# Linear attention into a mixture of experts on one core: rows kept whole per batch, one load for v's last tokens, an earlier choice of experts, and shifted tile addresses

## The chip, the core and the metric

The kernel runs on one core of a Trainium2 chip. The metric is the time of one execution in device microseconds (us); less is better. Several runs were timed, and one more execution was recorded by the hardware profiler.

## What is computed

The reference has two halves. The first is attention with a feature map, for 8 batches of 8 heads with 576 tokens and a head size of 64; the second sends the resulting 4608 rows of 512 numbers to one of 8 experts each.

```python
def phi(x):                                   # (.., 64) -> (.., 256)
    proj = x @ w_phi                          # 64 -> 128
    proj = proj - max(abs(proj))              # over the 128
    return concat([exp(proj), exp(-proj)])
kv = phi(k)^T @ v;  z = sum over tokens of phi(k)
attn = (phi(q) @ kv) / (phi(q) @ z + 1e-6)    # per batch and head
x = attn as rows of (batch, token), 512 wide
out = x.copy()
for rows with x @ w_skip > 0:                 # the others stay as they are
    e = argmax(x @ w_gate);  g = softmax(x @ w_gate)[e]
    out += g * (relu(x @ w1[e]) @ w2[e])      # w1: 512x1024, w2: 1024x512 per expert
```

## The kernel before

**Attention.** The work is cut into 16 units: a unit is four heads of one batch (`hq` is 0 or 1, `b` the batch), once for k and once for q. A loop over steps `t` from 0 to 38 runs a software pipeline: step 2g loads unit g, and each unit takes two steps. Within a step, the letters of `CFG['order']` say in which order projections (L336), maxima and subtractions (L346, L347 on VectorE, giving `m` and `u`), exponentials (L361, L378 on ScalarE), the products with v (L417, into `ps_K`) and the products of q with the result (L482, L535) are written. In the steps between `CFG['man']` that is the order on TensorE, VectorE, ScalarE and GpSimd; outside them, and for the DMA queue of SyncE (SP) throughout, a scheduler sets it. Each engine and each queue works strictly in its order.

**Loads.** For each unit SP issues four loads of v (L301, tile `v`, one buffer), four of k (L289), eight of q (L293), and four small ones with tokens 16 and 17 of each row of v straight into the tile `vt` (L308). GpSimd copies `v` into `vm` (L312), where a column of ones makes z.

**Rows and their choice of expert.** `norm` (L457 to L467) divides and writes two things: the rows, in `xm` (512 tokens) and `xt` (the last tokens of a pair of batches), and partial scores in `lgm`, `lgt`. There is one `xm` for each half row (`hq`). `store_rows` writes it to the scratch array `xrows`, `store_out` to the output. `post(b)` then works through a batch's choice in stages that are put off by whole steps: `best`, `exps`, `hot`, `gates` (which writes token number and gate into the last two columns of the row, L605 and L607), `store_rows`; then `rank`, `index`, `store_out`. Helpers put off in this way wait in `later` and are run at the letters L and R.

**Early experts.** After the sixth batch (`EB` is 5) `pick(0)` and `pick(1)` (from L700) take the two fullest experts so far; their numbers go to `eid`, their rows are gathered by GpSimd (L217, tile `xg`), and SP can issue the first loads of expert weights (L188 for w1, L191 for w2, tile `wraw_c`). ScalarE copies each block of weights (L199), and GpSimd or VectorE takes the remainder (L204). After attention come ten groups of expert slots; the tables for all but the first three are made once every batch has been ranked (L1068).

Of the kernel before, what the change touches and what calls it, by code (L numbers as in the profile page):

```python
# [20 lines left out]
CFG = {'late': 1, 'gp': (0, 1, 2, 4, 6, 8, 9, 11, 12, 14, 17, 19, 21), 'rows': 9.0, 'tab': (2, 4, 5, 6, 6, 7, 8, 9, 10, 11, 12, 13, 16, 20, 32), 'ql': 0, 'cp': 0, 'seq': ('E', 'E', 'E', 'C', 'C', 'SC', 'C', 'DS', 'C', 'D'), 'post': (2, 4, 1), 'man': (3, 36), 'eng': ('PE', 'DVE', 'Activation', 'Pool'), 'nb': {'K': 1, 'O': 1, 'A': 2, 'P': 3, 'U': 2}, 'apools': (('ld', 2), ('hl', 4), ('up', 5), ('zp', 2), ('ep', 7), ('kvp', 5), ('ac', 1), ('xp', 3)), 'mpools': (('rawp', 1), ('mx', 2), ('wseta', 1), ('mo', 2), ('wsetb', 1), ('wsetc', 1), ('rawq', 1)), 'lag': (2, 2, 3, 0), 'order': ('Lv12KQebRcdBuExzwl', 'L01aKQ2ebRcdBuExwzy'), 'vl': 0, 'at': 1, 'eb': (2, 2), 'ub': 4, 'stage': (1, 1, 2, 2), 'dve': ('0', '1', 'ntkq', '2', 'n2', 'tkq', 'n2t'), 'pd': 1, 'vq': 0, 'qq': 1, 'xb': 4, 'whole': 'k'}
# [3 lines left out]
def kernel(  # L25
# [106 lines left out]
    mark = const.tile([1, 32], I32, name="mark")[:, 0:1]  # L132
# [98 lines left out]
    with actx:  # L231
# [65 lines left out]
        def st_loadv(u):  # L297
            u.v0 = ld.tile([P, 4, 4 * D], F32, tag="v", name="v", bufs=1)
            u.vt = vts[u.g % len(vts)]
            for q4 in range(4):  # L300
                nc.sync.dma_start(  # L301
                    out=u.v0[q4 * 32:q4 * 32 + 32].rearrange("p h (t c) -> p h t c", c=D),
                    in_=vv[u.g][:, :, 4 * q4:4 * q4 + 4, :],
                )
            for pr in range(2):
                for q2 in range(2):
                    r = pr * 64 + q2 * 32
                    (nc.scalar if CFG["vq"] else nc.sync).dma_start(out=u.vt[r:r + 32, pr, :, 0:D], in_=vv[u.g][:, 2 * pr:2 * pr + 2, 16 + q2, :])  # L308

        def st_v(u):  # L310
            u.v = vms[u.g % len(vms)]
            nc.gpsimd.tensor_copy(out=u.v[:, :, :, 0:D], in_=u.v0.rearrange("p h (t c) -> p h t c", c=D))  # L312

# [157 lines left out]
        def st_use_q(u, pr, th):  # L471
            if th == 0:
                u.os = xp.tile([P, 8, NAUG], F32, tag="os", name="os", bufs=2)
            kva = kva_of[u.g]
            ov = bank("O")[:, 0:4 * NAUG].rearrange("p (t c) -> p t c", c=NAUG)
            e = u.e[pr]
            h0 = u.hq * 4 + 2 * pr
            for j in range(2):
                for hd in range(2):
                    for half in range(2):  # L480
                        for s in range(2):
                            nc.tensor.matmul(  # L482
                                ov[s * 64:s * 64 + 64, 2 * j + hd, :], e[:, half, s, 4 * hd + 2 * th + j],
                                kva[:, half, 2 * pr + hd, :], start=(half == 0), stop=(half == 1),
                            )
            nc.scalar.activation(out=u.os[:, 4 * th:4 * th + 4], in_=ov, func=AF.Copy)  # L486
            if th == 0:
                return
            if pr == 0:

# [4 lines left out]

            def finish():
                if pr == 0:
                    return
# [6 lines left out]
            norms.append(norm(u.os, 8, xm[:, :, pr * 2 * D:(pr + 1) * 2 * D].rearrange("p a (h d) -> p a h d", d=D),  # L505
                              lgm[:, :, h0:h0 + 2, :], 4) + [finish])

        def store_rows(b, hq):
# [1 line left out]
            nc.sync.dma_start(out=rowm[b][:, :, c], in_=xm_of[b * NQ + hq])  # L510
            if b % 2 == 1:
                nc.sync.dma_start(out=rowt[b // 2][:, c], in_=xt_of[b // 2, hq][:, 0])

        def store_out(b, hq):
            c = slice(hq * 4 * D, (hq + 1) * 4 * D)
            for q4 in range(4):
                rr = slice(q4 * 32, q4 * 32 + 32)
                nc.sync.dma_start(out=outv[b][:, q4 * 4:q4 * 4 + 4, c], in_=xm_of[b * NQ + hq][rr, :, 0:4 * D])
            if b % 2 == 1:
                for par in range(2):  # L520
                    for q2 in range(2):
                        rr = slice(par * 64 + q2 * 32, par * 64 + q2 * 32 + 32)
                        nc.sync.dma_start(out=outv[b - 1 + par][:, 16 + q2, c], in_=xt_of[b // 2, hq][rr, 0, 0:4 * D])
# [27 lines left out]
        def post(b):  # L551
            last = b == B - 1
            xm, lgm = xm_of[b * NQ + 1], lg_of[b]
            t0 = 9 * (b // 2) + 4 * (b % 2)
# [48 lines left out]
            def gates():  # L603
                for xx, lg, o, n in parts:
                    nc.scalar.activation(  # L605
                        out=xx[:, :, HW[1] - 1:HW[1]], in_=sid[:, t0 + o:t0 + o + n].rearrange("p (t o) -> p t o", o=1), func=AF.Copy)
                    nc.vector.reciprocal(out=xx[:, :, HW[1] - 2:HW[1] - 1], in_=gt[:, o:o + n].rearrange("p (t o) -> p t o", o=1))  # L607

            if last:
# [140 lines left out]
        for t in range(NPR + F + LQ + 2):  # L750
# [36 lines left out]
            for c in CFG["order"][t % 2]:  # L787
# [603 lines left out]
```

## Time and profile before

| | |
|---|---|
| times of three runs | 634.76 us median, 632.61 to 641.91 |
| the profiled execution | 632.63 us, of which the span of instructions is 630.9 us |
| mean granted TensorE clock | 0.947 |
| busy share | TensorE 85%, VectorE 71%, ScalarE 54%, GpSimd 48% |
| moved by DMA | 117.38 MB in 158466 packets |

The span is the time from the first to the last instruction of the core; some 1.7 us of the execution lie around it. In rows of the profile, PE is TensorE, PEld its weight loads, DVE VectorE, ACT ScalarE, POOL GpSimd, and SPq the DMA queue that SyncE issues. L301 is line 301 of the kernel before. A row of waits names who waited, for whom, the sum in us, how often, and the longest. In a timeline each row has the start and the length in us, the instruction, how many were merged, and in brackets the idle time ahead of it with what ended it.

### The profile page before, as it was taken

The page shows a single profiled execution, that of the slowest core. Times are in us where ns is not written, and L with a number is a line of the kernel's source. Part 1 is how long each engine was busy: PE and PEld are TensorE (multiplying, and loading weights), DVE is VectorE, ACT ScalarE, POOL GpSimd, SP SyncE. Part 2 cuts the span into 40 slices and gives each one's busy share as a digit, 9 for nine tenths or more (in the row PEclk, how much of TensorE's full clock was granted, in tenths as well). Part 3 has the DMA queues.
Part 4 walks back from the last instruction along what each step waited for, and adds up shares of the span by engine and source line. Part 5 has one row for each costly group of instructions (what it writes and reads, how often), then busy time and mean ns, then how long its engine had stood idle before and what let it go on. Part 6 is the DMA issues. An engine that isn't in the chain of part 4 may idle for free. (4 is left out here: it accounts for less than half of the span.)

```text
span 630.9 us, 20820 instructions
## 1 busy us (share of the span) xinstructions
PE 539.2 (85%) x8638; PEld 498.9 (79%) x8638; DVE 448.5 (71%) x781; ACT 341.7 (54%) x574; POOL 305.1 (48%) x502
## 2 busy tenths in 40 slices
PE   2679999888988869888975888879999988999994
PEld 2679899878987869787875777669988968888893
DVE  3687788876867847776755389986787788857751
ACT  1257677656754647566545353434567755664720
POOL 3112233535425144343246955996386956559021
PEclk9789999998998979989888798979999999999998
DMA  7877777777877688858734967478767788767500
GB/s 150 178 155 149 152 166 146 153 199 161 197 160 164 153 176 175 199 124 180 189 101 135 316 186 267 136 242 267 229 202 239 241 291 282 245 219 266 205 19 28
DMA packets 158466, 117.38 MB, mean 186 GB/s; under 512 B 88355, under 2 KB 139683, under 8 KB 158370
## 3 DMA queue, kind: packets, MB, share of 16 engines
q1 hardware_dynamic: 150304, 105.93, 63.9%
q0 software_dynamic: 3200, 9.45, 4.3%
q8 instruction: 69, 1.13, 0.8%
q10 hardware_dynamic: 4866, 0.66, 0.7%
q14 instruction: 27, 0.22, 0.1%
HBM read 92.77 MB, written 24.02 MB: 185 GB/s over the span
## 5 line engine op out<-in xcount | busy, mean ns | idle before, releaser
L204 POOL TENSOR_TENSOR w<-wraw_c,w 128x256 fp32r<-128x256 f32 x124 | 116.8, 973 | 35.4 <-ACT w L199 35.3
L346 DVE TENSOR_REDUCE m<-ps_A 128x8 f32<-128x1024 f32 x64 | 77.1, 1204 | 59.1 <-PE ps_A L336 59.1
L199 ACT ACTIVATE w<-wraw_c 128x1024 fp32r<-128x1024 f32 x96 | 98.1, 1051 | 20.2 <-DMA wraw_c<-in_moe_w_dram 20.1
L204 DVE TENSOR_TENSOR w<-wraw_c,w 128x1024 fp32r<-128x1024 f32 x65 | 85.9, 1333 | 11.4 <-ACT w L199 11.1
L336 PE MATMUL ps_A<-wsrc,xT 64*128 64x128 f32 x1024 | 80.8, 309 | 14.5 <-DVE u L347 13.1
L336 PEld LDWEIGHTS ps_A<-wsrc,xT 64*128 64x128 f32 x1024 | 73.1, 217 | 17.4 <-DVE u L347 13.3
L482 PE MATMUL ps_O<-kva,eq 128*64 128x74 f32 x2048 | 81.3, 233 | 5.9 <-ACT os L486 5.9
L417 PE MATMUL ps_K<-vm,ek 128*64 128x65 f32 x2048 | 79.6, 223 | 3.9 <-ACT ek L361 2.7
L347 DVE TENSOR_TENSOR u<-ps_A,m 128x1024 f32<-128x1024 f32 x64 | 78.4, 1225 | 4.0
L482 PEld LDWEIGHTS ps_O<-kva,eq 128*64 128x64 f32 x2048 | 72.8, 140 | 10.3 <-ACT os L486 6.1
L378 ACT ACTIVATE eq<-ps_V 128x1024 f32<-128x1024 f32 x64 | 65.7, 1028 | 21.5 <-PE ps_V L369 21.5
L417 PEld LDWEIGHTS ps_K<-vm,ek 128*64 128x64 f32 x2048 | 72.9, 140 | 4.8 <-issue 4.0
L1015 PE MATMUL ps_O<-w,hh 128*128 128x512 f32 x160 | 64.4, 403 | 2.5 <-DVE o L962 2.5
L361 ACT ACTIVATE ek<-u 128x1024 f32<-128x1024 f32 x64 | 64.1, 1056 | 2.3 <-DVE u L347 2.3
L948 POOL DMA_INDIRECT out_dram<-o,si x22 | 29.9, 1358 | 55.8 <-DVE si L947 49.2
L486 ACT ACTIVATE os<-ps_O 128x296 f32<-128x296 f32 x64 | 26.8, 419 | 46.8 <-PE ps_O L482 46.4
L312 POOL COPY vm<-v 128x1024 f32<-128x1024 f32 x16 | 16.6, 1037 | 71.2 <-DMA v<-in_v_dram 59.6
L1019 PE MATMUL ps_O<-w,hh 128*128 128x512 f32 x120 | 48.0, 400 | 3.2 <-POOL w L204 3.2
L1020 PE MATMUL ps_O<-w,hlo 128*128 128x512 f32 x120 | 47.6, 397 | 0.0
L465 POOL TENSOR_TENSOR xm<-os,rec 128x512 f32<-128x512 f32 x32 | 33.4, 1044 | 18.6 <-DVE rec L464 18.0
L1002 PE MATMUL ps_P<-x,w 128*128 128x256 f32 x144 | 37.1, 290 | 4.7 <-DVE x L879 4.7
L325 DVE STREAM_TRANSPOSE xT<-raw 128x512 f32<-128x512 f32 x64 | 40.4, 668 | 0.0
(269 smaller groups left out, 1106.2 us busy)
## 6 DMA issues: line engine op xcount, KB each, us to landing
wraw_c<-in_moe_w_dram SPq DMA_DIRECT2D x96, 512.0 KB, 4.6
raw<-in_k_dram SPq DMA_DIRECT2D x64, 280.0 KB, 5.8
raw<-in_q_dram SPq DMA_DIRECT2D x120, 72.0 KB, 5.1
v<-in_v_dram SPq DMA_DIRECT2D x64, 128.0 KB, 3.0
out_dram<-xm SPq DMA_DIRECT2D x64, 128.0 KB, 3.2
xrows<-xm SPq DMA_DIRECT2D x8, 516.0 KB, 5.0
xrows<-xm SPq DMA_DIRECT2D x8, 512.0 KB, 4.8
vt<-in_v_dram SPq DMA_DIRECT2D x64, 16.0 KB, 3.0
```

Source lines behind the costliest of these rows:

```text
L199: nc.scalar.activation(out=hi, in_=raw, func=AF.Copy)
L204: eng.tensor_tensor(out=lo[:, r], in0=raw[:, r], in1=hi[:, r].bitcast(F32), op=ALU.subtract)
L336: nc.tensor.matmul(p[:, hd, j * NF:(j + 1) * NF], xT[r], wsrc[r], start=True, stop=True)
L346: lambda: nc.vector.tensor_reduce(out=m, in_=pv, axis=AX.X, op=ALU.max, apply_absolute_value=True),
L347: lambda: nc.vector.tensor_tensor(out=uu, in0=pv, in1=m.rearrange("p h (j o) -> p h j o", o=1).broadcast_to([P, 2, n, NF]), op=ALU.subtract),
L361: nc.scalar.activation(out=o, in_=uu, func=AF.Exp, scale=(1.0, -1.0)[a])
L378: return [lambda a=a: nc.scalar.activation(out=e[:, a].rearrange("p s g c -> p s (g c)"), in_=t, func=AF.Exp, scale=(1.0, -1.0)[a]) for a ...
L417: nc.tensor.matmul(o[s * 64:s * 64 + 64, hd, half, :], e[:, half, s * 64:s * 64 + 64], x, start=(g == 0), stop=(g == 4))
L482: nc.tensor.matmul(ov[s * 64:s * 64 + 64, 2 * j + hd, :], e[:, half, s, 4 * hd + 2 * th + j], kva[:, half, 2 * pr + hd, :], start=(half == ...
L1015: nc.tensor.matmul(y[sub], hh[:, t], wh[:, fi, :], start=first, stop=False)
L1019: nc.tensor.matmul(y[sub], hh[:, t], wl[:, fi, :], start=False, stop=False)
L1020: nc.tensor.matmul(y[sub], hlo[:, t], wh[:, fi, :], start=False, stop=last)
```

## The change

1. **One tile of rows for each batch.** `xm` is 514 columns wide and allocated once per batch; `xt` likewise once per pair. A batch's rows go to `xrows` in one store (128 runs of 8,224 bytes in place of 1,024 runs of about 1 KB), and to the output in four stores in place of eight. Nothing is stored any more when only the first half is done.
2. **v's last tokens.** The four loads into `vt` become one load into a new tile `v1` on 32 partitions, and four GpSimd copies from there.
3. **Half steps.** `now` counts half steps, and a new letter `r` at the end of a step runs what is due there. All batches but the sixth keep their distances (`post` (4, 8, 2) for (2, 4, 1), and so on); the sixth has distances of its own: `post` starts half a step after its rows in place of a whole one, the stages follow after 1, 2, 3, 3 half steps (before 2, 2, 4, 4), rank, index and outputs after 3, 5, 2 (before 4, 8, 2), the two picks after 5 and 7 (before 10 and 12).
4. **The order by hand** holds to the end of step 37 (before 35).
5. **Addresses.** `mark` grows by 128 bytes per partition and a gap of 192 is put into the pool `mo`. In the built program the tiles that loads of k, q, v and weights write start at multiples of 256 bytes; before, they started 128 or 192 bytes past one.

```diff
-'post': (2, 4, 1), 'man': (3, 36), 'order': ('Lv12KQebRcdBuExzwl', 'L01aKQ2ebRcdBuExwzy'), 'stage': (1, 1, 2, 2)
+'post': (4, 8, 2), 'post2': (3, 5, 2), 'pk': (0, 2), 'man': (3, 38), 'order': ('Lv12KQebRcdBuExzwlr', 'L01aKQ2ebRcdBuExwzyr'), 'stage': (2, 2, 4, 4), 'stage2': (1, 2, 3, 3), 'vb': 1
-    mark = const.tile([1, 32], I32, name="mark")[:, 0:1]
+    mark = const.tile([1, 64], I32, name="mark")[:, 0:1]
...
+            u.v1 = ld.tile([32, 4, 2 * D], F32, tag="v1", name="v1", bufs=CFG["vb"])
+            nc.sync.dma_start(
+                out=u.v1, in_=vv[u.g][:, :, 16:18, :].rearrange("p h t c -> p h (t c)"))
...
             for pr in range(2):
                 for q2 in range(2):
                     r = pr * 64 + q2 * 32
-                    (nc.scalar if CFG["vq"] else nc.sync).dma_start(out=u.vt[r:r + 32, pr, :, 0:D], in_=vv[u.g][:, 2 * pr:2 * pr + 2, 16 + q2, :])
+                    nc.gpsimd.tensor_copy(
+                        out=u.vt[r:r + 32, pr, :, 0:D], in_=u.v1[:, 2 * pr:2 * pr + 2, q2 * D:(q2 + 1) * D])
...
-                xm_of[u.g] = xp.tile([P, 4, HW[u.hq]], F32, tag="xm%d" % u.hq, name="xm")
+                xm_of[u.b] = xp.tile([P, 4, XW], F32, tag="xm", name="xm")
...
-                if u.hq == 0:
-                    later.append((now[0] + 1, lambda: store_rows(u.b, 0), "R"))
-                    later.append((now[0] + 2, lambda: store_out(u.b, 0), "R"))
-                else:
-                    later.append((now[0] + CFG["pd"], lambda: post(u.b), "R"))
+                if pr == 1 and u.hq == 1:
+                    later.append((now[0] + (1 if u.b == EB else 2 * CFG["pd"]), lambda: post(u.b), "R"))
...
-            nc.sync.dma_start(out=rowm[b][:, :, c], in_=xm_of[b * NQ + hq])
+            nc.sync.dma_start(out=rowm[b], in_=xm_of[b])
...
-                nc.sync.dma_start(out=outv[b][:, q4 * 4:q4 * 4 + 4, c], in_=xm_of[b * NQ + hq][rr, :, 0:4 * D])
+                nc.sync.dma_start(out=outv[b][:, q4 * 4:q4 * 4 + 4], in_=xm_of[b][rr, :, 0:DM])
...
-                        later.append((now[0] + CFG["post"][1] + 1 + j, lambda j=j: pick(j), "L"))
+                        later.append((now[0] + CFG["post2"][1] + CFG["pk"][j], lambda j=j: pick(j), "L"))
...
+    mo.tile([1, 48], I32, tag="gap", name="gap", bufs=1)
```

Three places in the order of the built programs show what the change moves. (The changed kernel has line numbers of its own.)

**SP's queue in the middle of attention**, from one unit's loads of v to the next odd batch's stores. Before:

```order
L301 DMA v<-in_v_dram 32x4x256 x4
L289 DMA raw<-in_k_dram 32x2x1120 x4
L293 DMA raw<-in_q_dram 32x18x32 x8
L510 DMA xrows<-xm 512x1x256
L518 DMA out_dram<-xm 32x4x256 x4
L308 DMA vt_109<-in_v_dram 32x2x64 x2
L510 DMA xrows<-xm 512x1x258
L523 DMA out_dram<-xt 32x256 x4
L308 DMA vt_107<-in_v_dram 32x2x64 x2
L301 DMA v<-in_v_dram 32x4x256 x4
```

With the change:

```order
L300 DMA v<-in_v_dram 32x4x256 x4
L306 DMA v_3840<-in_v_dram 32x4x128
L288 DMA raw<-in_k_dram 32x2x1120 x4
L292 DMA raw<-in_q_dram 32x18x32 x8
L513 DMA out_dram<-xm 32x4x512 x4
L300 DMA v<-in_v_dram 32x4x256 x4
L306 DMA v_4235<-in_v_dram 32x4x128
L288 DMA raw<-in_k_dram 32x2x1120 x4
L292 DMA raw<-in_q_dram 32x18x32 x8
L506 DMA xrows<-xm 128x2056
```

Between two loads of v stood 26 other DMAs and now stand 17 in the one unit and, in the other, the loads and one store of rows (`v_3840` and `v_4235` are the new tile `v1`).

**VectorE at the first pick** (`eid` is the expert's number, `m` and `u` belong to attention). Before, the pick followed the last `m` and `u` of attention:

```order
L464 RECIPROCAL rec<-den 128x4
L346 TENSOR_REDUCE m<-ps_A 128x8
L347 TENSOR_TENSOR u<-ps_A,m 128x1024
L706 TENSOR_REDUCE mx<-ps_K 128x1
L707 TENSOR_TENSOR d<-ps_K,mx 128x8
L708 SCALAR_TENSOR_TENSOR key<-d,desc 128x8
L709 TENSOR_REDUCE km<-key 128x1
L710 TENSOR_TENSOR pks<-key,km 128x8
L711 TENSOR_SCALAR eid_137<-km 1x1
```

With the change:

```order
L329 STREAM_TRANSPOSE xT<-raw 128x4x4x32 x2
L350 TENSOR_REDUCE m<-ps_A 128x8
L351 TENSOR_TENSOR u<-ps_A,m 128x1024
L701 TENSOR_REDUCE mx<-ps_K 128x1
L702 TENSOR_TENSOR d<-ps_K,mx 128x8
L703 SCALAR_TENSOR_TENSOR key<-d,desc 128x8
L704 TENSOR_REDUCE km<-key 128x1
L705 TENSOR_TENSOR pks<-key,km 128x8
L706 TENSOR_SCALAR eid_137<-km 1x1
```

Four pairs of a full `m` and `u` now come behind the first pick, and none did before. The second pick moved with it: two pairs come behind it.

**ScalarE at the sixth batch's gates** (`xm<-sid` and `xt<-sid` write the token numbers). Before:

```order
L605 ACTIVATE xm<-sid 128x4
L605 ACTIVATE xt<-sid 128x1
L486 ACTIVATE os<-ps_O 128x296
L378 ACTIVATE eq<-ps_V 128x1024
L605 ACTIVATE xt<-sid 128x1
L424 ACTIVATE kva<-ps_K 128x2x2x65
L486 ACTIVATE os<-ps_O 128x296
```

With the change:

```order
L600 ACTIVATE xm<-sid 128x4
L600 ACTIVATE xt<-sid 128x1 x2
L490 ACTIVATE os<-ps_O 128x296
L382 ACTIVATE eq<-ps_V 128x1024
L490 ACTIVATE os<-ps_O 128x296
L428 ACTIVATE kva<-ps_K 128x2x2x65
```

The first `xt<-sid` is the sixth batch's; the second belongs to the eighth batch and writes the same single buffer of `xt`. It stood two instructions behind, and now follows at once.

More of the change, by code (lines that the diff above doesn't have):

```diff
@@ L20 @@
 SLOT = 256
[L21 removed]
+CFG = {'late': 1, 'gp': (0, 1, 2, 4, 6, 8, 9, 11, 12, 14, 17, 19, 21), 'rows': 9.0, 'tab': (2, 4, 5, 6, 6, 7, 8, 9, 10, 11, 12, 13, 16, 20, 32), 'ql': 0, 'cp': 0, 'seq': ('E', 'E', 'E', 'C', 'C', 'SC', 'C', 'DS', 'C', 'D'), 'post': (4, 8, 2), 'post2': (3, 5, 2), 'pk': (0, 2), 'man': (3, 38), 'eng': ('PE', 'DVE', 'Activation', 'Pool'), 'nb': {'K': 1, 'O': 1, 'A': 2, 'P': 3, 'U': 2}, 'apools': (('ld', 2), ('hl', 4), ('up', 5), ('zp', 2), ('ep', 7), ('kvp', 5), ('ac', 1), ('xp', 3)), 'mpools': (('rawp', 1), ('mx', 2), ('wseta', 1), ('mo', 2), ('wsetb', 1), ('wsetc', 1), ('rawq', 1)), 'lag': (2, 2, 3, 0), 'order': ('Lv12KQebRcdBuExzwlr', 'L01aKQ2ebRcdBuExwzyr'), 'vl': 0, 'at': 1, 'eb': (2, 2), 'ub': 4, 'stage': (2, 2, 4, 4), 'stage2': (1, 2, 3, 3), 'dve': ('0', '1', 'ntkq', '2', 'n2', 'tkq', 'n2t'), 'pd': 1, 'vq': 0, 'qq': 1, 'xb': 4, 'whole': 'k', 'vb': 1}
 @with_exitstack
@@ L297, in st_loadv @@
         def st_loadv(u):
-            u.v0 = ld.tile([P, 4, 4 * D], F32, tag="v", name="v", bufs=1)
+            u.v0 = ld.tile([P, 4, 4 * D], F32, tag="v", name="v", bufs=CFG["vb"])
             u.vt = vts[u.g % len(vts)]
@@ L605, in gates @@
                     nc.scalar.activation(
[L606 to L607 removed]
+                        out=xx[:, :, XW - 1:XW], in_=sid[:, t0 + o:t0 + o + n].rearrange("p (t o) -> p t o", o=1), func=AF.Copy)
+                    nc.vector.reciprocal(out=xx[:, :, XW - 2:XW - 1], in_=gt[:, o:o + n].rearrange("p (t o) -> p t o", o=1))
             if last:
@@ L613, in post @@
                 gates()
-                store_rows(b, 1)
+                store_rows(b)
             else:
                 best()
-                for dt, f in zip(CFG["stage"], (exps, hot, gates, lambda: store_rows(b, 1))):
+                for dt, f in zip(CFG["stage2" if b == EB else "stage"], (exps, hot, gates, lambda: store_rows(b))):
                     later.append((now[0] + dt, f, "R"))
@@ L684, in rest @@
             def rest():
-                store_out(b, 1)
+                store_out(b)
             if last:
@@ L689, in post @@
             else:
-                for dt, f, c in zip(CFG["post"], (rank, index, rest), "LLR"):
+                for dt, f, c in zip(CFG["post2" if b == EB else "post"], (rank, index, rest), "LLR"):
                     later.append((now[0] + dt, f, c))
@@ L755 @@
                 man.close()
-            now[0] = t
+            now[0] = 2 * t
             if t == CFG["at"]:
@@ L848 @@
                         st_logits(ukl)
-                elif c in "LR":
-                    for x in [x for x in later if x[0] <= t and x[2] == c]:
+                elif c in "LRr":
+                    if c == "r":
+                        now[0] = 2 * t + 1
+                    for x in [x for x in later if x[0] <= now[0] and x[2] == c.upper()]:
                         later.remove(x)
```

38 lines of the change are left out of this document (16 added, 22 removed).

## The prediction

> **What bounds the kernel now.** I first cut the span into stages, then attention into pairs of units, from one copy of v (L312) to the next but one. The columns are the stretch and its length, busy time of PE, PEld, DVE, ACT and POOL (with instructions), granted clock, DMA share, GB/s.
>
> ```profile
> 61.59:96.54 34.95, 32.22 (x864) 30.95 (x861) 28.27 (x40) 24.44 (x42) 11.81 (x25) 1.00 0.78 166
> 96.54:139.74 43.20, 39.55 (x1063) 38.25 (x1063) 35.93 (x62) 27.82 (x51) 15.97 (x36) 1.00 0.71 161
> 139.74:179.31 39.57, 35.52 (x900) 34.21 (x898) 30.11 (x53) 25.00 (x46) 16.83 (x37) 0.96 0.78 176
> 179.31:223.28 43.97, 35.66 (x898) 33.89 (x893) 30.86 (x53) 25.14 (x46) 16.16 (x36) 0.96 0.74 167
> 223.28:265.44 42.16, 36.22 (x910) 35.00 (x911) 29.95 (x52) 24.96 (x46) 16.79 (x37) 0.92 0.80 179
> 265.44:305.70 40.26, 33.30 (x752) 31.61 (x749) 27.18 (x50) 22.94 (x42) 16.18 (x37) 0.87 0.73 164
> 550.00:600.00 50.00, 49.67 (x298) 44.09 (x298) 34.22 (x49) 30.91 (x47) 26.69 (x30) 1.00 0.70 233
> ```
>
> A pair with hardly any stores takes 34.95 us. Once stores have begun, five pairs take 209.16 us, 41.8 each, though PE's matmuls grow only to 4523 in five, 904.6 each. No engine is full there. The queue that SP issues is; here is its timeline over a pair of units:
>
> ```profile
> 195.72 1.79 SPq L301 DMA_DIRECT2D v<-in_v_dram  x4
> 197.61 1.78 SPq L289 DMA_DIRECT2D raw<-in_k_dram  x4
> 199.50 8.23 SPq L293 DMA_DIRECT2D raw<-in_q_dram  x8
> 207.83 0.58 SPq L510 DMA_DIRECT2D xrows<-xm  x1
> 208.46 3.14 SPq L518 DMA_DIRECT2D out_dram<-xm  x4
> 212.01 0.79 SPq L308 DMA_DIRECT2D vt<-in_v_dram  x2
> 212.92 1.43 SPq L510 DMA_DIRECT2D xrows<-xm  x1
> 214.45 2.46 SPq L523 DMA_DIRECT2D out_dram<-xt  x4
> 217.01 0.84 SPq L308 DMA_DIRECT2D vt<-in_v_dram  x2
> 217.95 2.99 SPq L301 DMA_DIRECT2D v<-in_v_dram  x4
> 221.04 1.78 SPq L289 DMA_DIRECT2D raw<-in_k_dram  x4
> 222.92 8.18 SPq L293 DMA_DIRECT2D raw<-in_q_dram  x8
> 231.20 2.02 SPq L518 DMA_DIRECT2D out_dram<-xm  x4
> 233.32 1.86 SPq L308 DMA_DIRECT2D vt<-in_v_dram  x4
> ```
>
> One row begins where the last ends: SP issues for 39.5 us (195.72 to 235.18) without a rest. From 41.56 to 305.7 its waits are twenty small rows, 15.7 us together, the largest this first one; below it stands what the late loads do to the engines in the same stretch:
>
> ```profile
> SPq L510 <- ACT ek L361: 2.3, 2, 1.3
> POOL vm L312 <- DMA v<-in_v_dram: 57.7, 11, 9.9
> PE ps_A L336 <- DVE u L347: 13.1, 9, 2.9
> PE ps_V L369 <- POOL kvs L429: 9.1, 6, 2.0
> PE ps_K L629 <- POOL OH L600: 5.4, 4, 2.5
> ```
>
> POOL stands 57.7 us at the copy of v, and in its order `OH` and `kvs` come behind that copy; PE then waits for those two. So SP's list of DMAs sets the pace of the pairs, and PE (92% busy in the free pair, 83% from 265 to 305, clock down to 0.87) is next. In the expert stage PE is full: 49.67 of 50 us. Between the two lies the handover:
>
> ```profile
> PE ps_O L482 <- ACT os L486: 5.9, 2, 5.3
> PE ps_K L1068 <- DVE Stot L651: 3.6, 1, 3.6
> PE ps_O L535 <- ACT os L486: 2.0, 1, 2.0
> 339.83 2.17 SPq L188 DMA_DIRECT2D wraw_c<-in_moe_w_dram  x4
> 343.57 1.06 ACT L199 ACTIVATE w<-wraw_c 128x1024 fp32r<-128x1024 f32 x1 [3.94 <-DMA wraw_c<-in_moe_w_dram]
> 349.04 1.06 ACT L199 ACTIVATE w<-wraw_c 128x1024 fp32r<-128x1024 f32 x1 [2.25 <-DMA wraw_c<-in_moe_w_dram]
> 340.00:350.00 10.00, 3.42 (x41) 2.87 (x41) 3.84 (x18) 4.18 (x5) 8.89 (x14) 0.62 0.91 280
> ```
>
> The first weights are issued at 339.83 us, behind the pick; ACT waits 3.94 and 2.25 us for them with `os` queued behind, and PE stands 5.3 and 2.0 us; the clock in that window is 0.62.
>
> **The change in the pairs.** I price SP's list from its rows, per pair. The small loads into `vt`, eight in 0.79 + 0.84 + 1.86 = 3.49 us, become two of 64 KB, between a `vt` and a `v` load in size; at 1.79/4 = 0.45 us each that is 0.9, so 2.6 less. Two stores to `xrows` (0.58 + 1.43) become one of 128 runs, priced at 0.5: 1.5 less. The stores from `xt` halve: 2.46 to 1.23, 1.2 less. The output stores from `xm` (3.14 + 2.02 = 5.16 for eight) become four with the same bytes. If only issuing counts they halve, if the transfers hold the queue back they cost the same; I take 3.6, in between, 1.5 less. SP's list falls from 39.5 to about 32.7 us, below what PE needs.
>
> PE's need: 904.6 matmuls at the free pair's 32.22/864 us are 33.7 us busy; at its 92% that pair would take 36.6 us. I take 38.0, about 89%, because POOL's list gets longer. The copies of 32x128 that it gains are not in the trace; nearest are these:
>
> ```profile
> L142 POOL COPY wgd<-wgs x2: 208/212/216, 25.1 to 25.4; 64x36 f32<-64x36 f32 x2
> L429 POOL COPY kvs<-kva 128x256 f32<-128x256 f32 x32 | 12.7, 397 | 24.5 <-ACT kva L424 24.3
> ```
>
> Between 212 and 397 ns by length gives about 0.29 us, 1.2 us a unit for four, 18.6 us in all. POOL is busy 16.16 of 43.97 us in a pair, so its idle time hides them while v comes in time; without that cover each unit would pass 1.2 us on to `OH` and `kvs`. The term is 5 x (41.8 - 38.0) = **19 us** gained. Its bounds are 26 (36.6 us a pair) and 13, the latter from the transfers: the highest share of a pair is 0.80, and 41.8 us at the five pairs' mean of 0.75 holds 31.4 us of DMA work, which at 0.80 takes 39.3. Before 61 us there are next to no stores; I count nothing there.
>
> Here a page of the Trainium skill speaks against the change: "DMA: Bandwidth & Descriptors", section "Issuing engines are not separate DMA queues", says that the issue time of a DMA is usually small beside the DMA itself. By that rule fewer issues of the same bytes would bring little, and the pairs' term would be near 0, which is the second rival below; the rows differ from it, since the two `vt` loads at 212.01 hold the queue 0.79 us for 32 KB, while four loads of v with 512 KB took 1.79.
>
> **The change at the handover.** On DVE the pick's number is the third row here; in the order of the change it comes between the first two:
>
> ```profile
> 307.43 1.23 DVE L347 TENSOR_TENSOR u<-ps_A,m 128x1024 f32<-128x1024 f32 x1
> 311.82 1.22 DVE L346 TENSOR_REDUCE m<-ps_A 128x8 f32<-128x1024 f32 x1 [3.17 <-PE ps_A L336]
> 338.67 0.13 DVE L711 TENSOR_SCALAR eid<-km 1x1 int32<-1x1 f32 x1
> ```
>
> That is 27 to 30 us earlier. The first weights came 3.7 us after their issue (339.83 to 343.57), so the four loads are now there long before ACT asks for them. ACT's 3.94 and 2.25 us go. What is late next is ACT itself: four copies of 1.06 us now stand in one block ahead of `os`, 4.2 us where the first wait and copy took 4.9. So of PE's 5.3 and 2.0 us I take back 3. POOL's four gathers leave 340 to 350, where POOL is 8.89 of 10 us busy and where the last batches' `den`, `xm` and `Stot` queue; I give 2 of the 3.6 us that PE waits for `Stot`. With a shorter pause I count 2 us for the clock.
>
> Against it stand two waits. The denser stages of the sixth batch bring PE to `rank` and `index` sooner behind POOL's `OH`, on which each late one has cost 5.4/4 = 1.3 us: 1 us lost. And ACT's second `xt<-sid` waits for the store of the only `xt` buffer:
>
> ```profile
> ACT xt L605 <- DMA xrows<-xt: 3.9, 1, 3.9
> PE ps_K L441 <- ACT kva L424: 3.7, 1, 3.7
> ```
>
> These 3.9 us became 3.7 on PE before, with `os` and `eq` done in between. Now it stands right behind the sixth batch's gates, and the store that it waits for can be issued only behind those gates and behind a store of twice the size, with `os`, `eq` and `kva` queued after it on ACT. I take 5 us of PE's time, 1 more than before; it could be 8 more if SP is still issuing q then. Sum of the handover: 3 + 2 + 2 - 1 - 1 = **5 us** gained, between 12 gained (all three PE waits and 1 us of clock) and 5 lost.
>
> The tile addresses change loads alone. The row at 550 shows PE full at a DMA share of 0.70, so that is worth 0 in the expert stage; bounds 2 either way for the handover. The longer order by hand is priced within the handover's bounds.
>
> On the addresses, the Trainium skill ("DMA: Bandwidth & Descriptors", section "How a descriptor splits into AXI transactions") says that a transaction must start at a multiple of 256 bytes, so that a run of 1 KB begun 128 bytes off takes five and not four. By it the first weights would land up to a fifth sooner, under 1 us of the 3.7, and the sum would be 1 us lower; no run yet shows it.
>
> **Rivals.** *Transfers take the place of issues*: as in the lower bound, the output stores cost what they did and pairs settle at 39.3 us; 13 + 5 us gained would give 615. For it: the same four loads of v held the queue 1.79 us once and 2.99 us the other time, so more than issuing is in these rows. Against it: the share was only 0.71 in a pair of 43.2 us, which no shortage of transfers made long. *The shorter list brings nothing*: if the pairs' pace is really PE waiting on VectorE (13.1 us, the largest of its rows), only the handover's 5 us remain: 628. Against it: the free pair ran at 92% PE with the same chain. *Slower*: POOL becomes what PE waits for. If v is still late in most units, the four copies land behind it and ahead of `OH` and `kvs`, and all sixteen units pay 1.2 us; with 19 us lost, nothing gained in the pairs and the handover's 5 us lost too, 657. It decides when POOL's wait at v stays near 57.7 us. *The early pick does not bring the weights early*, since SP's first weight load still has q's loads and the sixth batch's stores ahead of it: the handover turns from 5 gained to 5 lost, 619.
>
> **How the numbers follow.** The execution profiled took 632.63 us (span 630.9 and 1.7 around it), 2 us under the median of 634.76. The forecast is 632.6 - 19 - 5 = **608 us**. Chances: the forecast with its own spread (600 to 616) 0.55; transfers instead of issues or no early weights (613 to 621) 0.23; nothing from the list (623 to 632) 0.13; slower 0.05; better than both bounds together (under 597) 0.04. The range reaches from 597 (632.6 less 26, the pairs' whole bound, and 9, most of the handover's) to 624, which takes in the two rivals next to the forecast and a part of the third. A measurement of this kernel can tell about 2% from no change, 622 and 647 around the median: faster 0.80 (the second case ends at the edge and gives 0.02 away), the same 0.15, slower 0.05.
>
> **What would show it.** Pairs of some 38 us with PE near 90% and a clock near 1.00; rows of SP waiting for engines in place of an unbroken issue; POOL's wait at the copy of v under 20 us and PE's rows for `kvs` and `OH` nearly gone; weight loads issued at least 20 us ahead of the last `m`, no ACT wait for `wraw_c` at the first copies; one ACT wait for `xrows<-xt` of 5 us or more with PE standing behind it. The prediction is wrong if SP still issues without a rest at 41 us a pair, if POOL still waits for v, or if the gain sits in the expert stage.

## The result and the profile after

With the change the kernel takes 604.9 us (median of four runs, 602.23 to 605.79), against 634.19 us before, measured beside it (632.61 to 641.91). The ratio is 0.952, with a 95% interval of 0.947 to 0.957: 30 us faster. The forecast was 608 us, with a range of 597 to 624.

The pairs of units come first again, cut at every second copy of v as in the prediction (length, then busy time of PE, PEld, DVE, ACT and POOL, granted clock, DMA share, GB/s). These are the five pairs that took 209.16 us before.

```profile
92.78:127.69 34.91, 33.27 (x885) 32.07 (x885) 29.35 (x53) 24.20 (x46) 18.18 (x43) 1.00 0.80 187
127.69:164.96 37.27, 33.43 (x893) 32.13 (x892) 30.97 (x53) 24.70 (x47) 19.13 (x46) 1.00 0.85 195
164.96:201.59 36.63, 33.50 (x887) 32.28 (x887) 30.16 (x52) 24.60 (x46) 18.43 (x44) 1.00 0.85 195
201.59:240.54 38.95, 34.76 (x894) 33.64 (x894) 30.07 (x52) 24.81 (x47) 19.17 (x45) 0.96 0.84 192
240.54:277.00 36.46, 33.41 (x893) 32.35 (x893) 30.38 (x54) 24.86 (x49) 19.75 (x49) 1.00 0.79 187
```

They now take 184.2 us, 36.8 each, with 4452 matmuls where the five before held 4523, since the cuts follow GpSimd's copies and not PE. PE's matmuls are busy for 168.4 of it (91%), and the clock is at 1.00 in four of the five. SP's timeline over one pair of units in the changed kernel, from one load of v to the next but one:

```profile
168.39 3.65 SPq L300 DMA_DIRECT2D v<-in_v_dram  x4
172.14 0.38 SPq L306 DMA_DIRECT2D v<-in_v_dram  x1
172.61 2.50 SPq L288 DMA_DIRECT2D raw<-in_k_dram  x4
175.22 7.29 SPq L292 DMA_DIRECT2D raw<-in_q_dram  x8
182.62 0.56 SPq L506 DMA_DIRECT2D xrows<-xm  x1
183.69 3.49 SPq L518 DMA_DIRECT2D out_dram<-xt  x4
187.28 2.92 SPq L300 DMA_DIRECT2D v<-in_v_dram  x4
190.30 0.39 SPq L306 DMA_DIRECT2D v<-in_v_dram  x1
190.78 1.79 SPq L288 DMA_DIRECT2D raw<-in_k_dram  x4
192.67 8.24 SPq L292 DMA_DIRECT2D raw<-in_q_dram  x8
201.00 4.13 SPq L513 DMA_DIRECT2D out_dram<-xm  x4
```

The loads of the last tokens (0.38 us each) and the one store of rows (0.56 us) are as short as they were priced. The rest is longer than in the estimate: four output stores hold the queue 4.13 us where I had 3.6, v's four loads 2.92 and 3.65 us, and the four stores from `xt`, which come in every second pair, 3.49 us. In this pair SP's rows add up to 35.3 us of 36.8. Summed over all five pairs, SP's timeline has 33.3 us of rows a pair, where it had 40.3 before, and its pauses of over 0.2 us add up to 9.0 us, where they were 0.4. So the list is now shorter than the pairs, and SP rests in between. The waits of the changed kernel from 41 to 300 us (who waited, for whom, sum, times, longest) tell the same from the engines' side:

```profile
PE ps_O L486 <- ACT os L490: 5.6, 1, 5.6
PE ps_A L340 <- DVE u L351: 4.3, 6, 1.0
PE ps_V L373 <- POOL kvs L433: 1.4, 2, 0.7
PE ps_K L624 <- POOL OH L595: 1.0, 1, 1.0
ACT xt L600 <- DMA xrows<-xt: 7.4, 1, 7.4
```

PE's waits for `kvs` and `OH` fell from 9.1 and 5.4 us to 1.4 and 1.0, those for `u` from 13.1 to 4.3, and no row of POOL waiting for v is left where 57.7 us stood. In the first row ScalarE's wait for the store from `xt`, the last row, reaches PE, since `os` is queued behind it.

The two profiled spans differ by 27.7 us (630.9 and 603.2). To see where these came from I cut both traces at `eq`, of which there are 64 in either, so that each stretch ends at the same point of the same work: from the 8th to the 48th, the 56th and the 64th, and on to TensorE's table product behind `Stot`. Before, then after:

```profile
64.99:261.03 196.04, 172.27 (x4426) 165.79 (x4422) 148.48 (x250) 123.69 (x225) 76.25 (x169) 0.97 0.75 167
261.03:306.50 45.47, 37.82 (x893) 35.98 (x890) 31.32 (x55) 25.09 (x48) 16.98 (x37) 0.89 0.76 171
306.50:344.83 38.33, 27.80 (x720) 26.36 (x714) 20.74 (x58) 21.12 (x43) 18.85 (x42) 0.92 0.46 123
344.83:380.47 35.64, 29.07 (x276) 25.79 (x277) 22.45 (x65) 17.13 (x26) 28.15 (x42) 0.84 0.79 239
```

```profile
60.37:245.15 184.78, 169.20 (x4426) 163.04 (x4423) 148.68 (x250) 123.05 (x225) 88.94 (x211) 0.98 0.83 189
245.15:287.88 42.73, 34.27 (x917) 33.06 (x912) 34.81 (x67) 25.15 (x51) 24.43 (x57) 0.99 0.65 166
287.88:324.25 36.37, 28.70 (x688) 26.74 (x688) 17.66 (x51) 23.59 (x41) 16.91 (x35) 0.92 0.39 118
324.25:353.83 29.58, 26.48 (x277) 23.72 (x278) 18.99 (x58) 11.10 (x21) 20.51 (x32) 0.94 0.70 223
```

The start gave 4.6 us (64.99 to 60.37), the long middle 11.3, the next stretches 2.7, 2.0 and 6.1; behind `Stot` hardly anything changed (250.4 and 249.4 us to the end of the span). The counts in brackets warn that the second stretch has 24 more matmuls after than before, since the early pick brings its rank and index forward: the last three stretches must be read together, 119.4 us before and 108.7 after.

### The profile page after: what moved, and what is told of

Same layout as the page of the kernel before. It is cut to its first block, busy times and chain, and to the rows that moved or that the text cites. A ratio compares the mean times of both kernels' runs of the same rounds, so it can differ in the third digit from the quotient of the medians.

```text
span 603.2 us, 20741 instructions
## 1 busy us (share of the span) xinstructions
PE 530.0 (88%) x8638; PEld 490.4 (81%) x8638; DVE 445.0 (74%) x781; ACT 340.8 (57%) x574; POOL 326.5 (54%) x566
## 2 busy tenths in 40 slices
DMA packets 142402, 117.38 MB, mean 195 GB/s; under 512 B 82531, under 2 KB 117475, under 8 KB 141282
## 5 line engine op out<-in xcount | busy, mean ns | idle before, releaser
L204 POOL TENSOR_TENSOR w<-wraw_c,w 128x256 fp32r<-128x256 f32 x124 | 122.3, 1020 | 39.0 <-ACT w L199 21.4
L350 DVE TENSOR_REDUCE m<-ps_A 128x8 f32<-128x1024 f32 x64 | 77.0, 1204 | 33.5 <-PE ps_A L340 33.3
L204 DVE TENSOR_TENSOR w<-wraw_c,w 128x1024 fp32r<-128x1024 f32 x65 | 88.6, 1374 | 14.9 <-ACT w L199 14.3
L486 PE MATMUL ps_O<-kva,eq 128*64 128x74 f32 x2048 | 82.2, 232 | 15.1 <-ACT os L490 10.4
L421 PE MATMUL ps_K<-vm,ek 128*64 128x65 f32 x2048 | 82.2, 226 | 6.2 <-issue 3.9
L421 PEld LDWEIGHTS ps_K<-vm,ek 128*64 128x64 f32 x2048 | 74.9, 142 | 7.9 <-issue 4.8
L340 PE MATMUL ps_A<-wsrc,xT 64*128 64x128 f32 x1024 | 72.7, 288 | 7.3 <-DVE u L351 6.0
L340 PEld LDWEIGHTS ps_A<-wsrc,xT 64*128 64x128 f32 x1024 | 65.5, 198 | 9.9 <-DVE u L351 5.5
L382 ACT ACTIVATE eq<-ps_V 128x1024 f32<-128x1024 f32 x64 | 65.8, 1029 | 12.3 <-PE ps_V L373 12.3
L365 ACT ACTIVATE ek<-u 128x1024 f32<-128x1024 f32 x64 | 64.1, 1056 | 8.2 <-DVE u L351 8.2
L948 POOL DMA_INDIRECT out_dram<-o,si x22 | 27.7, 1258 | 47.7 <-DVE si L947 40.7
L421 PE MATMUL ps_K<-vt,ekt 128*64 128x65 f32 x512 | 38.7, 227 | 0.0
```

The costliest lines, as they stand in the source:

```text
L204: eng.tensor_tensor(out=lo[:, r], in0=raw[:, r], in1=hi[:, r].bitcast(F32), op=ALU.subtract)
L340: nc.tensor.matmul(p[:, hd, j * NF:(j + 1) * NF], xT[r], wsrc[r], start=True, stop=True)
L350: lambda: nc.vector.tensor_reduce(out=m, in_=pv, axis=AX.X, op=ALU.max, apply_absolute_value=True),
L365: nc.scalar.activation(out=o, in_=uu, func=AF.Exp, scale=(1.0, -1.0)[a])
L382: return [lambda a=a: nc.scalar.activation(out=e[:, a].rearrange("p s g c -> p s (g c)"), in_=t, func=AF.Exp, scale=(1.0, -1.0)[a]) for a ...
L421: nc.tensor.matmul(o[s * 64:s * 64 + 64, hd, half, :], e[:, half, s * 64:s * 64 + 64], x, start=(g == 0), stop=(g == 4))
```

## The experiments

The theory to test: SP's list of DMA issues set the pace of the pairs, and the shorter list brought it down to PE's. Its rivals are that the transfers or the waits of ScalarE did, and that the early pick or the addresses brought part of the gain. Ratios are to the kernel before, run on the same chip beside each; the change itself stands at 0.952.

### v's last tokens loaded as before (e1_vt_loads)

```diff
-            nc.sync.dma_start(out=u.v1, in_=vv[u.g][:, :, 16:18, :].rearrange("p h t c -> p h (t c)"))
+                    nc.sync.dma_start(out=u.vt[r:r + 32, pr, :, 0:D], in_=vv[u.g][:, 2 * pr:2 * pr + 2, 16 + q2, :])
...
-                    nc.gpsimd.tensor_copy(out=u.vt[r:r + 32, pr, :, 0:D], in_=u.v1[...])
```

> The changed kernel with v's last tokens loaded as before: four loads straight into vt for each unit, no v1, no copies on GpSimd. My theory (SP's list of issues sets the pairs' pace once it is longer than PE's need of some 36.6 us): eight loads at 0.44 us in place of two at 0.38 make the list 2.7 us longer per pair, so pairs go from the changed kernel's 36.8 us to 38.5 to 39.5 and five pairs cost 9 to 13 us more: 613 to 618 us. Rival, transfers set the pace: no byte is added (only 128 more short runs per unit), so within 2 us of the changed kernel, 603 to 607. Rival, the copies on GpSimd are a cost: 1.2 us a unit come free, so 590 to 603.

621.6 us, ratio 0.977 (0.971 to 0.982): some 16 us lost, a little more than I expected; the copies on GpSimd cost less than the loads they replace. The place was not the expected one, however. The same two stretches as above, the middle and the one from the 48th to the 56th `eq`, in this run:

```profile
64.06:247.95 183.89, 166.92 (x4426) 161.13 (x4422) 148.11 (x249) 123.24 (x225) 76.63 (x169) 0.99 0.78 176
247.95:299.97 52.02, 37.59 (x917) 35.99 (x912) 35.35 (x68) 25.23 (x52) 23.48 (x50) 0.88 0.78 187
```

The middle is no longer than in the change's profile, though SP no longer rests in it (no pause is over 0.43 us); the short stretch grew from 42.7 to 52.0 us. Its waits and one row each of SP and ACT:

```profile
PE ps_O L482 <- ACT os L486: 11.2, 2, 6.1
ACT xm L596 <- issue: 5.6, 1, 5.6
277.82 0.36 SPq L502 DMA_DIRECT2D xrows<-xm  x1
282.06 0.21 ACT L596 ACTIVATE xm<-sid 128x4 f32<-128x4 f32 x1 [5.63 <-issue]
```

ScalarE stands 5.6 us at a write of token numbers into `xm`, besides the 7.5 us at the one into `xt`, and PE twice behind `os`. For the first of the two the profile names no releaser; that it waited for a store is argued from the order and the times. These two writes belong to the last batch. They lie outside the order by hand, and the scheduler has moved them ahead to the sixth batch's; rows 298 and 310 of ScalarE's order are the last batch's, the others the sixth's:

```
297 L588 ACTIVATE ex<-d 128x40
298 L600 ACTIVATE xm<-sid 128x4
308 L600 ACTIVATE xm<-sid 128x4
309 L600 ACTIVATE xt<-sid 128x1
310 L600 ACTIVATE xt<-sid 128x1
```

There they wait until the tiles they take over, the fifth batch's `xm` and the sixth's `xt`, have been stored. In this run the fifth batch's store to `xrows` was issued at 277.82 us, behind q's loads, in the changed kernel at 256.33. A longer list on SP thus becomes a wait of ScalarE; how much of the 16 us this is, a later run without these writes shows.

### Every store in two halves (e2_split_stores)

```diff
-            nc.sync.dma_start(out=rowm[b], in_=xm_of[b])
+            for c in (slice(0, 4 * D), slice(4 * D, XW)):
+                nc.sync.dma_start(out=rowm[b][:, :, c], in_=xm_of[b][:, :, c])
```

and the same for the stores to `rowt` and to the output.

> The changed kernel with each store of rows (xrows and output, xm and xt) issued as two stores of half rows at the same place in the program: twice the issues, the same bytes, and runs of about 1 KB as before. My theory (issues set the pace): the rows of before and after give 1.2 us more for xm's output stores, 1.4 for xrows and 1.2 for xt per pair, 3.8 us together: pairs of 39 to 41 us, 617 to 626 us. Rival, only bytes count: within 2 us of the changed kernel, 603 to 607.

618.0 us, ratio 0.968 (0.961 to 0.974), so 10 to 13 us lost at the same bytes. Again the middle did not grow, and the short stretch did:

```profile
62.06:243.50 181.44, 167.21 (x4426) 161.30 (x4422) 148.39 (x250) 122.89 (x225) 88.45 (x212) 0.99 0.82 181
243.50:294.46 50.96, 36.08 (x917) 34.52 (x911) 34.48 (x67) 25.21 (x51) 24.14 (x56) 0.91 0.77 174
```

Here ScalarE's wait at the early write into `xt` was 12.3 us against 7.4, and PE stood 10.1 us behind it. The time came out as expected, by another way.

### Both undone together (e7_both_lists)

The two edits above in one kernel.

> The changed kernel with both of the undone parts together: four loads straight into vt and each store of rows in two halves. Each alone left the five pairs between the 8th and the 48th eq at 181 to 184 us (178 to 185 with the change, 196 before) and cost 12 to 15 us in all, most of it where ScalarE waits for stores that SP issues late. My theory (SP's list sets the pace where it is longer than PE's need; each alone stays just under it): the list is 6.5 us longer per pair, the five pairs go to 190 to 198 us, in all 625 to 640 us. Rival, the list never set the pace of those pairs and only ScalarE's waits count: the five pairs stay at 178 to 186, in all 615 to 624 us.

640.9 us, ratio 1.007 (1.003 to 1.011), just above what I expected: all of the gain is gone. And now the middle is as long as before the change, at the same DMA share, with POOL late for v again:

```profile
63.54:261.04 197.50, 173.59 (x4426) 167.09 (x4422) 148.54 (x250) 123.53 (x226) 76.63 (x170) 0.96 0.75 166
POOL vm L312 <- DMA v<-in_v_dram: 37.0, 8, 7.6
```

SP issues without a pause of over 0.43 us, as it did before the change (0.41). So the list does set the pace once it is clearly longer than PE's need: either part alone leaves it about level, both together put it over. The rival by which only ScalarE's waits count is out, since it had the middle at 178 to 186 us. So is the one by which the transfers do, since the same bytes went at a share of 0.83 with the change.

### v in sixteen loads (e8_v_sixteen)

```diff
-                nc.sync.dma_start(out=u.v0[q4 * 32:q4 * 32 + 32]..., in_=vv[u.g][:, :, 4 * q4:4 * q4 + 4, :])
+                for h in range(4):
+                    nc.sync.dma_start(out=u.v0[q4 * 32:q4 * 32 + 32, h]..., in_=vv[u.g][:, h, 4 * q4:4 * q4 + 4, :])
```

> The changed kernel with v loaded by sixteen loads of one head each in place of four: 24 more issues per pair, the same bytes in the same runs of 1 KB. Issues by count (0.45 us each, from four loads of v in 1.79 us): SP's list grows by 10 us to 45 us a pair, the five pairs between the 8th and the 48th eq go from 178 to 185 us to 220 to 230, in all 645 to 665 us. Issues by what they carry (the time follows runs and bytes): no change, 603 to 608 us.

691.4 us, ratio 1.086 (1.079 to 1.093): 86 us for 192 more issues, with the same bytes (117.40 against 117.38 MB) and 2% more packets. The first two rows are v's issues in the change and in this run (times in ns, shortest, median and longest, then the first and last start in us); then come the middle stretch and the largest waits of POOL and PE from 60 to 300 us:

```profile
L300 SPq DMA_DIRECT2D v<-in_v_dram x64: 311/436/2342, 8.7 to 263.6; - x64
L301 SPq DMA_DIRECT2D v<-in_v_dram x256: 310/420/2181, 8.4 to 353.8; - x128
74.01:304.51 230.50, 186.06 (x4426) 179.37 (x4423) 148.69 (x250) 124.75 (x225) 88.68 (x210) 0.88 0.65 145
POOL vm L311 <- DMA v<-in_v_dram: 64.0, 9, 9.9
PE ps_V L373 <- POOL kvs L433: 26.3, 10, 4.9
```

A load of 32 KB holds the queue as long as one of 128 KB in the same runs of 1 KB, 0.42 and 0.44 us in the median, and single ones of either take over 2 us. In the middle sixteen in a row hold it for 10.4 to 10.9 us. The pairs take 46.1 us, and the chain of the prediction (v late, POOL at the copy, `kvs` behind it, PE) stands there enlarged, with transfers rarer than before (share 0.65). The total is above what I expected for issues, since I had priced the middle only: the start grew by 13.6 us, from 60.4 to 74.0, and the stretch behind the middle from 42.7 to 67.5.

### The late pick (e3_late_pick)

```diff
-'post2': (3, 5, 2), 'pk': (0, 2), 'man': (3, 38), 'stage2': (1, 2, 3, 3)
+'post2': (4, 8, 2), 'pk': (2, 4), 'man': (3, 36), 'stage2': (2, 2, 4, 4)
-                    later.append((now[0] + (1 if u.b == EB else 2 * CFG["pd"]), lambda: post(u.b), "R"))
+                    later.append((now[0] + 2 * CFG["pd"], lambda: post(u.b), "R"))
```

> The changed kernel with the sixth batch's stages at the distances of the other batches, its picks at the old places, and the order by hand to step 35 as before: the handover of before with the attention of after. The prediction's theory (the early pick and its neighbours bring 5 us): 608 to 612 us. The reading of the two traces (about 3 us of the wait for weights gained and given back in ACT's wait on the store from xt, in issues and in PE's wait for OH): 604 to 608, with ACT's waits on wraw_c back and PE's wait behind them of 5 us or more.

605.9 us, ratio 0.950 (0.944 to 0.955): the early pick and the longer order by hand bring nothing that these runs can tell. The four stretches with the late pick, whose matmul counts are those of before:

```profile
62.17:241.80 179.63, 166.22 (x4426) 160.24 (x4422) 148.59 (x250) 123.13 (x226) 88.57 (x211) 1.00 0.85 193
241.80:277.31 35.51, 33.15 (x893) 32.01 (x890) 29.98 (x53) 24.73 (x47) 18.35 (x45) 1.00 0.68 161
277.31:318.26 40.95, 29.09 (x720) 27.63 (x715) 21.90 (x59) 21.04 (x42) 18.38 (x41) 0.90 0.30 92
318.26:352.98 34.72, 28.80 (x276) 25.84 (x277) 21.50 (x65) 13.75 (x24) 25.06 (x38) 0.82 0.76 245
```

The last three are 111.2 us together, as they are in the next experiment, which has the early pick (44.1 + 36.4 + 30.7). The early pick shortens the last two by 8.6 us (4.6 and 4.0) and lengthens the first of the three by the same 8.6, in part because 24 matmuls move into it.

### Without the shifted addresses (e4_addresses)

```diff
-    mark = const.tile([1, 64], I32, name="mark")[:, 0:1]
+    mark = const.tile([1, 32], I32, name="mark")[:, 0:1]
-    mo.tile([1, 48], I32, tag="gap", name="gap", bufs=1)
```

> The changed kernel without the two gaps in the addresses, so that loads of k, q, v and weights start 128 or 192 bytes past a multiple of 256; the order of all engines is the same row for row. My theory (addresses are worth nothing here): 603 to 607 us, and the loads of wraw_c and v land as late as with the gaps, within 0.2 us. Rival, runs that start off 256 bytes cost one more transaction each: v's runs of 1 KB take up to a fifth longer, the DMA share of a pair rises from 0.83 to 0.9 or more and pairs lengthen by 1 to 3 us: 608 to 620 us.

606.1 us, ratio 0.951 (0.946 to 0.957): no difference from the change. The DMA table (KB each, median us from issue to landing), with the shifted addresses first, and without them followed by the four stretches:

```profile
wraw_c<-in_moe_w_dram SPq DMA_DIRECT2D x96, 512.0 KB, 5.2
v<-in_v_dram SPq DMA_DIRECT2D x64, 128.0 KB, 2.8
```

```profile
wraw_c<-in_moe_w_dram SPq DMA_DIRECT2D x96, 512.0 KB, 5.3
v<-in_v_dram SPq DMA_DIRECT2D x64, 128.0 KB, 3.2
63.19:241.18 177.99, 166.24 (x4426) 160.17 (x4423) 148.08 (x249) 122.98 (x225) 88.11 (x211) 1.00 0.84 193
241.18:285.30 44.12, 35.94 (x917) 34.62 (x912) 34.90 (x67) 25.13 (x52) 24.33 (x57) 0.94 0.65 166
285.30:321.70 36.40, 28.81 (x688) 26.73 (x688) 17.65 (x51) 23.57 (x41) 16.86 (x35) 0.92 0.38 118
321.70:352.37 30.67, 27.58 (x276) 24.63 (x277) 18.36 (x58) 11.50 (x22) 20.49 (x32) 0.91 0.69 217
```

v lands 0.4 us later without them, more than the 0.2 I allowed, but k lands no later (5.5 against 5.6), the DMA share of the middle is the same, and the middle was the shortest of all here. Profiles with the same list have it at 178.0, 179.6, 181.5 and 184.8 us (the change itself), which is how far such a stretch varies.

### The last batch's numbers written late (e5_late_sid)

```diff
+                    if last:
+                        nc.vector.scalar_tensor_tensor(
+                            out=xx[:, :, XW - 1:XW], in0=gt[:, o:o + n].rearrange("p (t o) -> p t o", o=1), scalar=0.0, in1=sc,
+                            op0=ALU.mult, op1=ALU.add)
+                    else:
                         nc.scalar.activation(out=xx[:, :, XW - 1:XW], in_=sc, func=AF.Copy)
```

> The changed kernel with one edit: the last batch's token numbers are written into its rows by VectorE from gt times 0 plus sid, so that the writing depends on the last batch's gates and can't be moved ahead; ScalarE's two early writes, which wait for the stores of the fifth batch's xm and the sixth batch's xt, are gone, all else stands in the same order. My theory: PE's wait of 5.6 us for os behind that write goes, the stretch from the 48th to the 56th eq falls from 42.7 to 44.1 us to 37 to 39, and 5 us come through to the end: 597 to 601 us. Rival, something else is late at once (the first copies of weights, Stot): 602 to 606 us.

599.4 us, ratio 0.941 (0.937 to 0.946), which lies wholly under the change's interval. The stretch from the 48th to the 56th `eq`:

```profile
241.87:278.05 36.18, 33.56 (x899) 32.42 (x895) 30.36 (x57) 25.03 (x50) 19.23 (x48) 1.00 0.68 162
```

36.2 us in place of 42.7, and the wait for `os` is gone. The last three stretches are 104.0 us together, where they were 108.7 and 111.2 with the early writes. This kernel is faster than the change.

### The late pick without those waits (e9_late_both)

The edits of the late pick on top of the last kernel.

> The kernel in which the last batch's token numbers are written late (599.4 us), with the sixth batch's stages, picks and the order by hand put back as before: what the early pick is worth by itself once ScalarE's wait on the stores is out of both. By the traces the late pick has ScalarE waiting for the first weights and PE standing 5.2 + 3.0 us at os, where the early one stands 4.2 us behind four copies in a row: 4 us more, 602 to 605 us. By the comparison of the late with the early pick that still had the wait in both (605.9 against 604.9 and 606.1): nothing, 598 to 601 us.

597.3 us, ratio 0.939 (0.932 to 0.947), not distinguishable from the 599.4: the early pick shows no worth here either. The last three stretches are 103.5 us together, against 104.0. PE's longest wait at `os`, behind ScalarE's first copies of weights, is 5.6 us in this run, where the early pick has 4.2.

### v's last tokens as before, without those waits (e12_vt_loads_late)

The edit of the first experiment on the kernel with the late write.

> The kernel in which the last batch's token numbers are written late (599.4 us), with v's last tokens loaded as before, four loads straight into vt for each unit. With ScalarE's early writes in place this undoing cost 15 us. If most of that was ScalarE waiting for stores that a longer list issues later (two waits of 5.6 and 7.5 us, PE 11.2 us behind them): 3 to 7 us are left, 602 to 607 us. If the longer list itself costs it, by PE waiting for v, kvs or OH: 611 to 616 us.

611.0 us, ratio 0.960 (0.952 to 0.968), 11.6 us over the 599.4. So most of the 16 us that the loads cost above is the list itself; some 4 us are left for ScalarE's waits, a difference within the spread of the runs. POOL waits 18.5 us for v again, PE 11.4 us for `u`, and the five pairs of the middle take 187.2 us against 181.5.

### Output stores issued by ScalarE (e10_out_act)

```diff
-                nc.sync.dma_start(out=outv[b][:, q4 * 4:q4 * 4 + 4], in_=xm_of[b][rr, :, 0:DM])
+                nc.scalar.dma_start(out=outv[b][:, q4 * 4:q4 * 4 + 4], in_=xm_of[b][rr, :, 0:DM])
```

on the kernel with the late write.

> The kernel in which the last batch's token numbers are written late (599.4 us), with the output stores from xm issued by ScalarE's queue in place of SP's: SP's list is 4 us shorter in each pair, the transfers are the same. My theory (with the change PE, not SP's list, sets the pairs' pace): the five pairs between the 8th and the 48th eq stay at 178 to 185 us, and ScalarE pays 2 to 4 us a batch for issuing, of which little reaches PE: 597 to 607 us. Rival, SP's list still sets the pace: the five pairs fall by 2 to 4 us each, in all 582 to 592 us.

603.3 us, ratio 0.949 (0.940 to 0.958): no faster. The middle takes 184.1 us (181.5 with the stores on SP), though SP has 5 us less of rows in each pair and pauses for 37 us in all. With the change SP's list no longer sets the pace. The four stores hold ScalarE for some 3.3 us a batch; how much of that reaches PE was not measured apart.

### The copies from v1 three times (e6_copies_x3)

```diff
+                    for _ in range(3):
                         nc.gpsimd.tensor_copy(out=u.vt[r:r + 32, pr, :, 0:D], in_=u.v1[...])
```

> The changed kernel with each of GpSimd's copies from v1 into vt done three times: eight more copies of 0.29 us for each unit, 37 us of GpSimd work in all, the same result. My theory (the copies lie in GpSimd's idle time): 603 to 609 us, GpSimd's busy time in a pair up by 4.6 us, PE's rows for kvs and OH a little larger, 1 to 3 us together. Rival, the copies stand ahead of kvs and OH and are paid by PE: 2.3 us a unit, 630 to 640 us.

616.0 us, ratio 0.969 (0.962 to 0.976): 11 us lost, between what the two theories gave, and each holds in a place of its own. The two windows are the start and the middle:

```profile
0.00:73.52 73.52, 45.10 (x922) 42.34 (x924) 41.61 (x58) 28.26 (x45) 26.31 (x98) 0.93 0.74 152
73.52:252.65 179.13, 165.79 (x4426) 159.69 (x4422) 148.44 (x250) 122.94 (x225) 111.55 (x291) 1.00 0.82 188
PE ps_V L374 <- POOL kvs L434: 8.0, 3, 4.6
```

In the middle 22.6 us more of GpSimd work (111.55 against 88.94) cost nothing. The start went from 60.4 to 73.5 us; the last row is from 10 to 75 us: the first copies of `kvs` stand behind copies into `vt` that wait for their load, and PE waits for them, 8.0 us of the 13.1 lost there. The single copies are hidden in the pairs; that they cost nothing at the start isn't shown.

## Why the prediction came out right, and where it was not

**The bound was named rightly.** SP's list set the pace: 192 more issues at the same bytes cost 86 us, and with both lists long again the middle is back at 197.5 us (196.0 before). A rule of the Trainium skill ("DMA: Bandwidth & Descriptors", section "Issuing engines are not separate DMA queues") says that the issue time is usually small beside the DMA itself. For a single load this case agrees: v's loads of 32 KB hold the queue 0.42 us and land 2.5 us after their issue (medians). But the issues of one queue stand one behind the other, and before the change 55 of them filled 40.3 us of a pair of 41.8.

**The pairs' term was too small.** I forecast 19 us, from 41.8 to 38.0 us a pair. Cut at v's copies as I did, the pairs came to 36.8 us, 25 us gained, close to the upper bound of 26. (The early pick lies partly in these pairs; with the late pick, whose stretches hold the same matmuls as before, the 8th to 56th `eq` went from 241.5 to 215.1 us, 26 us.) The step that failed is the choice of 38.0: I took 89% for PE for fear of POOL, and POOL's copies of 0.29 us each lay in its idle time. The list fell by what I had forecast, 7.0 us a pair (40.3 to 33.3) for 6.8, but not row by row: the stores from `xt` took 3.49 us in every second pair where I had 1.23 in each, and v's loads took 2.92 and 3.65 us where they had taken 1.79 and 2.99. That the longer rows wait for transfers is likely at shares of 0.79 to 0.85, but not shown. The rival of the transfers took 0.80 as the highest share; the pairs ran at 0.85.

**The start gave 4.6 us in this profile, forecast 0.** The other kernels with the same list reach the 8th `eq` at 60.3 to 63.2 us, so 2 to 5 us were gained. I had argued that next to nothing is stored there; with the loads of the last tokens put back the 8th `eq` was at 64.1 and 63.4 us. It is not settled further.

**The handover's 5 us did not come.** This is the failed step. The weights were early, as forecast (issued at 295.91 us, with ScalarE's four copies of 3.88 us in one block from 320.17 on), and PE's wait at `os` behind them is 4.2 us: 3 gained. ScalarE's wait on the store from `xt` was 7.4 us with PE standing 5.6 behind it, as forecast within a microsecond. Of the wait for `Stot` I took back 2 us and got 0.8 (3.6 to 2.8). The clock rose too (0.91 and 0.94 in the last stretch ahead of the table product, 0.82 with the late pick). What the sum put at nothing is that the pause moves: with ScalarE's early writes gone from both, the early pick shortens that stretch by 3.2 us (29.7 against 32.9) and lengthens the one before it by 4.4 (38.2 against 33.8). Why that one grows is open. In all the early pick gains nothing, with those writes (604.9 against 605.9 us) or without them (599.4 against 597.3 us).

That the time came out only 3 us under the forecast is in part luck: the two errors, 6 us too little in the pairs and 5 too much at the handover, nearly cancel, and the start adds its few.

**Addresses: 0 forecast, 0 found.** By the Trainium skill's rule of 256 bytes ("DMA: Bandwidth & Descriptors", section "How a descriptor splits into AXI transactions") my estimate had the weights land up to a fifth sooner with the shifted addresses; they landed in 5.2 us against 5.3 without. In the kernel before, also without, it was 4.6.

**Of the signs** I had named, POOL's wait at v, PE's rows for `kvs` and `OH`, the clock, and the `xt` wait came as said. Two came in part: SP rests for 9.0 us in the five pairs but still issues for nine tenths of them, and the weights were issued 18 us, not 20, ahead of the last `m` (at 314.0).

## What to carry to other kernels

Read the queue of an issuing engine like any other engine: add up its rows over one period of the loop and compare the sum with the busiest engine's. If it is longer, cut the number of DMAs, not the bytes, and stop when the two are level, since beyond that nothing came here (603.3 against 599.4 us). Then look in the order for instructions that have been moved ahead and wait for a buffer to be stored: on a strict queue such a write makes every delay of a store a stall of everything behind it, and giving it a data dependency that keeps it late was worth 5.5 us here.

## What the runs showed that I had not expected

- **An issue's price does not follow its bytes.** In the median v's loads of 128 KB hold SP's queue for 0.44 us, those of 32 KB for 0.42 and k's of 280 KB for 0.42; q's of 72 KB, in runs of 128 bytes, take 0.63. The longest issue of each kind takes 1.7 us or more; why is open.
- **PE's clock was lower where it waited more.** The 4426 matmuls of the middle are the same in three of the kernels. They took 166.2 us at a clock of 1.00, 172.3 at 0.97 and 186.1 at 0.88, where PE idled 12, 24 and 44 us between them. So of the 52 us that separate the longest middle from the shortest, 20 are PE's own work at a lower clock. That idling lowers the clock is read from the rows, not tried by itself.
- **A late store reached PE through ScalarE.** With v's last tokens loaded as before, the fifth batch's rows were stored 21 us later (277.82 against 256.33), and the stretch after the middle grew by 9 us. With the early writes gone, the same loads lengthen it by 2.4 us (36.2 to 38.6).
